# A gated unit's last weights: how its rows are split between a plain load and a gather, and how the gather's pieces are dealt to the DMA engines

## The chip, the cores and the metric

The kernel runs on one core of a Trainium2 chip. Times are device microseconds of one execution. The core has a matrix engine (TensorE, "PE" in the profile, with "PEld" for its weight loads), a vector engine (VectorE, DVE), a scalar engine (ScalarE, ACT), GpSimd (POOL) and SyncE (SP). Data comes from HBM into SBUF, which has 128 partitions, through 16 DMA engines that all queues share.

## The reference

A decode step for eight sequences, D = 512. The row `x` is normalised, then goes into attention over a window of 2048 cached positions (32 query heads, 8 key-value heads of 128) and into a gated unit with F = 1792; the attention's output is scaled by a function of the unit's.

```python
xn = _layernorm(x)                                   # x: 8 x 1 x 512
# A: attention over the last W = 2048 of 8192 positions
q = (xn @ wq) -> 32 heads of 128;  k, v = k_cache[:, :, Sk-W:], v_cache[:, :, Sk-W:]
p = softmax(q . k * 128 ** -0.5);  s = (p . v) @ wo  # wq 512 x 4096, wo 4096 x 512
# B: the gated unit
g = xn @ w_gate;  u = xn @ w_up                      # 512 x 1792 each
b = (sigmoid(g) * u) @ w_down                        # w_down 1792 x 512
out = x + s * silu(b)
```

All data is bfloat16. The caches' windows are 64 MB of the 81 MB that are read.

## The kernel before

One buffer, `ring` (L86), holds nine slots of 16 KB a partition. Every large load goes into slots of it, and all are issued by SP in one order, the list `todo`: a load is issued when a slot is free (`pump`, L89), and `free` (L103) gives slots back when the last reader of a load is recorded. The order is w_gate in two loads, w_up, the last rows of w_down (`want_down`), the gathered rows of w_down (`want_side`), wq, 17 drains of SP's queue, then 32 loads of K and V of 2 MB each (`want_cache`, one sequence and four heads a load, V three loads behind K), then wo in four loads of 16, 10, 4 and 2 rows a partition (`want_rows`).

A load with 128 partitions is split over the 16 DMA engines by partition, eight partitions each, so each engine gets the same bytes of every plain load. w_down is the exception. Its 1792 rows of 1 KB are read in two ways:

- `want_down` (L156) reads the last MT x 128 rows, MT rows to each partition, as one plain load.
- `want_side` (L145) only takes a slot and sets its first SF rows in all partitions to zero (L148, on DVE). The first 64 x SF rows are 64 pieces of SF rows, which one gather by GpSimd (L239) puts into 64 of the 128 partitions. Each partition has an index in `which`; those without a piece have one that is out of bounds, and nothing is read for them.

Which partitions get a piece is said by `SEGS`: triples of first partition, count and step (L139). `sel` (L211 to L219), a 64 x 128 matrix of zeros and ones, is made from them on GpSimd, a copy for each triple; a matmul with `ranks` turns it into the indices (L229 to L238).

The unit is computed at the start: `g_ps` (L323) and `u_ps` (L339) on PE, `h_bf` on DVE (L346), then MT + SF transposes of it (L358), MT of 128 rows and SF of 64. The transposed columns of the pieces are brought to the pieces' partitions by a matmul with `sel` (`spot_ps`, L398), and MT + SF matmuls `d_ps` (L403) give the unit's output, the partitions without a piece adding zeros. In between stand the projection `q_ps` (L387) and after it the heads' layout (L417 to L422).

Then the loop over sequences: K tiles are transposed on PE (`kT_ps`, L484) and copied by DVE (L489), scores (`s_ps`, L502), softmax, transposes of p (L591), values (`o_ps`, L612). At the end 32 steps of four matmuls `fin_ps` (L372) with wo's rows, two DVE operations (L756, L758) and the store by SP and ACT (L760).

Of the kernel before, what the change touches and what calls it, by code (L numbers as in the profile page):

```python
# [10 lines left out]
def kernel(  # L11
# [91 lines left out]
    def free(t):  # L103
        empty.extend(t[1])
        pump()

    def room(k, n, *shape):
        size = 1
        for x in shape:
            size *= x  # L110
        x = ring[:, k : k + n].rearrange("p s e -> p (s e)")[:, :size]
        if len(shape) == 2:
            x = x.rearrange("p (r n) -> p r n", r=shape[0])
        return x, list(range(k, k + n))
# [18 lines left out]

        todo.append((n, f))

    MT = 9
    SF = 10
    NSEL = 64
    SEGS = [(0, 15, 1), (16, 3, 1), (28, 18, 1), (48, 2, 1)]  # L139
    SEGS += [(60, 8, 1), (68, 6, 4), (92, 8, 1), (124, 4, 1)]  # L140
    m0 = NSEL * SF
    assert sum(n for _, n, _ in SEGS) == NSEL and m0 + MT * P == F
    side = {}

    def want_side(w):  # L145
        def f(k):
            t, where = room(k, 1, SF, w.shape[1])
            nc.vector.memzero(t)  # L148
            side["t"] = t
            rows_of[("side", 0)] = (t, where)  # L150
            for r in range(SF):
                weights[("wd_sb", MT + r)] = t[:, r]

        todo.append((1, f))

    def want_down(w):  # L156
        def f(k):
            t, where = room(k, 1, MT, w.shape[1])
            q0.dma_start(
                out=t.rearrange("p t n -> p (t n)"),  # L160
                in_=w[m0:, :].rearrange("(p t) n -> p (t n)", t=MT),
            )
            rows_of[("wd_sb", 0)] = (t, where)
            for r in range(MT):
                weights[("wd_sb", r)] = t[:, r, :]
# [47 lines left out]
    at = 0  # L213
    for p, n, step in SEGS:
        nc.gpsimd.tensor_copy(
# [25 lines left out]
        out_offset=None,  # L241
        in_=B_w_down[:m0, :].rearrange("(p t) n -> p (t n)", t=SF),
        in_offset=bass.IndirectOffsetOnAxis(ap=which[:, :1], axis=0),
# [42 lines left out]

    hT_sb = work.tile([P, MT + SF, Z], bf16, name="hT_sb")
    nc.gpsimd.memzero(hT_sb[:])
# [63 lines left out]
    free(rows_of[("wu_sb", 0)])  # L352
    hT_ps = ps_m.tile([P, MT + SF, B], bf16, name="hT_ps", tag="m")
    cuts = [h_bf[:B, m0:F].rearrange("b (p t) -> b t p", t=MT)[:, t] for t in range(MT)]
# [441 lines left out]
```

## Time and profile before

| | us |
|---|---|
| median of 3 runs | 198.49 (198.38 to 198.54) |
| the profiled execution's own time | 198.86 |
| its span, first to last instruction | 197.08 |
| PE busy | 163.4 |
| DVE busy | 125.7 |
| ACT busy | 40.8 |
| POOL busy | 9.1 |
| mean granted TensorE clock | 0.972 of full |
| bytes read | 81.67 MB, 414 GB/s over the span |

The profile is of one execution, so its durations are summed against that execution's own time. Stages are given in microseconds from the span's start. Beside the page, the trace holds a record of every DMA packet (queue, start, duration, bytes) and of every step of a DMA's completion semaphore, sixteen for a load, one from each DMA engine; neither says which of the sixteen it was.

### The profile page before, as it was taken

The page shows a single profiled execution, that of the slowest core. Times are in us where ns is not written, and L with a number is a line of the kernel's source. Part 1 is how long each engine was busy: PE and PEld are TensorE (multiplying, and loading weights), DVE is VectorE, ACT ScalarE, POOL GpSimd, SP SyncE. Part 2 cuts the span into 40 slices and gives each one's busy share as a digit, 9 for nine tenths or more (in the row PEclk, how much of TensorE's full clock was granted, in tenths as well). Part 3 has the DMA queues.
Part 4 walks back from the last instruction along what each step waited for, and adds up shares of the span by engine and source line. Part 5 has one row for each costly group of instructions (what it writes and reads, how often), then busy time and mean ns, then how long its engine had stood idle before and what let it go on. Part 6 is the DMA issues. An engine that isn't in the chain of part 4 may idle for free.

```text
span 197.1 us, 4818 instructions
## 1 busy us (share of the span) xinstructions
PE 163.4 (83%) x2114; PEld 106.8 (54%) x2114; DVE 125.7 (64%) x247; ACT 40.8 (21%) x95; POOL 9.1 (5%) x31
## 2 busy tenths in 40 slices
PE   0029859999699999799979987999799998878883
PEld 0013423876576575456646654665467566655652
DVE  4540401999799796679667966796549878935201
ACT  0053003001701501600160016001600070071000
POOL 7910000000000000000000000000000000000000
PEclk9999966999999999999999999999879999999999
DMA  6999999999999999999999999999999999999990
GB/s 203 438 440 463 416 406 426 436 436 432 424 429 429 422 426 422 439 432 432 426 432 434 426 426 421 429 436 426 419 442 439 426 431 422 426 429 429 420 401 16
DMA packets 6148, 81.32 MB, mean 413 GB/s; under 512 B 808, under 2 KB 816, under 8 KB 1328
## 3 DMA queue, kind: packets, MB, share of 16 engines
q1 hardware_dynamic: 5936, 80.35, 96.0%
q0 software_dynamic: 144, 0.66, 0.8%
q8 instruction: 16, 0.26, 0.5%
q14 instruction: 4, 0.03, 0.0%
q10 hardware_dynamic: 48, 0.01, 0.0%
HBM read 81.67 MB, written 0.01 MB: 414 GB/s over the span
## 4 chain that ended last, share of the span: by engine, by line
DMA 65%; PE 25%; DVE 5%; ACT 3%; issue 1%; SPq 0%; ACTq 0%
DMA ring<-in_A_k_cache_dram 29%; DMA ring<-in_A_v_cache_dram 13%; PE kT_ps L484 13%; DMA ring<-in_A_wq_dram 11%; DMA ring<-in_A_wo_dram 10%; PE s_ps L502 4%; PE o_ps L612 3%; DMA ring<-in_B_w_gate_dram 3%; DVE kT_sb L489 2%; PE q_ps L387 2%; ACT p_buf L522 2%; PE fin_ps L372 1%; PE d_ps L403 1%; DVE pT_sb L596 1%; ACT L522 1%
## 5 line engine op out<-in xcount | busy, mean ns | idle before, releaser
L489 DVE COPY kT_sb<-kT_ps 128x1024 bf16<-128x1024 bf16 x128 | 84.3, 684 | 26.0 <-PE kT_ps L484 21.2
L484 PE MATMUL kT_ps<-perm,ring 128*128 128x128 bf16 x1024 | 73.4, 221 | 2.0 <-DMA ring<-in_A_k_cache_dram 2.0
L484 PEld LDWEIGHTS <-ring 128*128 128x128 bf16 x1024 | 59.5, 99 | 24.6 <-issue 18.3
L612 PE MATMUL o_ps<-ring,pT_sb 128*32 128x256 bf16 (+1 forms) x352 | 36.6, 330 | 6.6 <-DMA ring<-in_A_v_cache_dram 5.6
L502 PE MATMUL s_ps<-kT_sb,qm_sb 128*32 128x512 bf16 x256 | 25.8, 393 | 1.3 <-DVE kT_sb L489 1.1
L522 ACT ACTIVATE p_buf<-s_ps,st 32x512 bf16<-32x512 f32 x32 | 21.7, 679 | 15.5 <-DVE st L515 15.1
L612 PEld LDWEIGHTS <-pT_sb 128*32 128x32 bf16 (+1 forms) x352 | 12.4, 102 | 19.4 <-issue 17.6
L632 ACT ACTIVATE o_sb<-o_ps,fac 128x512 f32<-128x512 f32 (+1 forms) x8 | 4.9, 608 | 60.5 <-PE o_ps L612 60.5
L596 DVE COPY pT_sb<-pT_ps 128x1024 bf16<-128x1024 bf16 x16 | 10.8, 676 | 1.8 <-PE pT_ps L591 1.8
L502 PEld LDWEIGHTS <-qm_sb 128*32 128x32 bf16 x256 | 7.0, 93 | 8.1 <-issue 1.5
L591 PE MATMUL pT_ps<-turn_rows,p_buf 128*128 128x128 bf16 x128 | 10.7, 227 | 0.0
L591 PEld LDWEIGHTS <-p_buf 128*128 128x128 bf16 x128 | 9.4, 148 | 0.2 <-issue 0.2
L278 PE MATMUL xnT_ps<-ident,xn_bf 8*128 8x8 bf16 x4 | 0.3, 174 | 9.9 <-DVE xn_bf L267 9.9
L549 ACT ACTIVATE w_row<-w 1x128 f32<-1x128 f32 x8 | 2.5, 308 | 28.6 <-DVE w L542 28.6
L346 DVE TENSOR_TENSOR h_bf<-sig,u_ps 8x448 bf16<-8x448 f32 x4 | 2.4, 608 | 6.6 <-PE u_ps L339 6.1
L422 DVE COPY qm_sb<-qT_ps 128x128 bf16<-128x128 bf16 x2 | 1.4, 876 | 8.1 <-PE qT_ps L417 8.1
L323 PE MATMUL g_ps<-ring,xnT_sb 128*8 128x448 bf16 x16 | 5.7, 541 | 0.3 <-DVE xnT_sb L285 0.3
L522 ACT ACTIVATION_READ_ACCUMULATOR p_buf<-s_ps,st 32x1 f32 x32 | 5.9, 184 | 0.0
L515 DVE TENSOR_REDUCE st<-s_ps 128x1 f32<-128x512 f32 x8 | 5.5, 682 | 0.5 <-PE s_ps L502 0.5
L278 PEld LDWEIGHTS <-xn_bf 8*128 8x128 bf16 x4 | 0.2, 114 | 10.0 <-DVE xn_bf L267 10.0
L387 PE MATMUL q_ps<-ring,xnT_sb 128*32 128x512 bf16 x32 | 3.6, 629 | 2.4 <-DMA ring<-in_A_wq_dram 2.4
L642 PE MATMUL m_ps<-ident_f,o_sb 128*128 128x32 f32 x40 | 5.2, 272 | 0.0
(97 smaller groups left out, 97.0 us busy)
## 6 DMA issues: line engine op xcount, KB each, us to landing
ring<-in_A_k_cache_dram SPq DMA_DIRECT2D x16, 2048.0 KB, 28.5
ring<-in_A_v_cache_dram SPq DMA_DIRECT2D x16, 2048.0 KB, 30.4
ring<-in_A_wq_dram SPq DMA_DIRECT2D x1, 4096.0 KB, 21.6
ring<-in_A_wo_dram SPq DMA_DIRECT2D x1, 2048.0 KB
ring<-in_B_w_gate_dram SPq DMA_DIRECT2D x2, 896.0 KB, 6.0
ring<-in_B_w_up_dram SPq DMA_DIRECT2D x1, 1792.0 KB, 13.1
ring<-in_A_wo_dram SPq DMA_DIRECT2D x1, 1280.0 KB
ring<-in_B_w_down_dram SPq DMA_DIRECT2D x1, 1152.0 KB
```

The costliest lines, as they stand in the source:

```text
L323: nc.tensor.matmul(g_ps[:], lhsT=xnT_sb[:, kt, :B], rhs=weights[("wg_sb", kt)][:, k * FC : (k + 1) * FC], start=(kt == 0), stop=(kt == KT ...
L387: nc.tensor.matmul(q_ps[e][Z * g : Z * (g + 1), :], lhsT=xnT_sb[:, kt, :], rhs=weights[("wq_sb", kt)][:, c0 : c0 + D], start=(kt == 0), st ...
L484: nc.tensor.transpose(out=kT_ps[:, c, :], in_=k_sb[:, j * CU + h * CH + c, :], identity=perm[:],)
L489: nc.vector.tensor_copy(out=kT[(b, u)][:, h * CH : (h + 1) * CH, :], in_=kT_ps[:])
L502: nc.tensor.matmul(s_ps[b][NR * l : NR * (l + 1), :], lhsT=qm_sb[:, b, i * G + l, o : o + Z], rhs=t[:, :, PG * l : PG * (l + 1)], start=(u ...
L515: nc.vector.tensor_reduce(out=st[b][:], in_=s_ps[b][:], axis=AX.X, op=ALU.max, negate=True)
L522: nc.scalar.activation(out=p_buf[b % 2][rows, :, l, :], in_=s[rows, :].rearrange("k (c p) -> k p c", p=PG), func=AF.Exp, bias=st[b][rows, ...
L591: nc.tensor.transpose(out=pT_ps[:, c, :], in_=p_buf[b % 2][:, :, :, h * CH + c].rearrange("k p l -> k (p l)"), identity=turn_rows[:],)
L596: nc.vector.tensor_copy(out=pT[b][:, h * CH : (h + 1) * CH, :], in_=pT_ps[:])
L612: nc.tensor.matmul(o_ps[r] if b < WIDE else o_ps[r, 0:2], lhsT=pT[b][:, c, r], rhs=x, start=(c == 0), stop=(c == CU - 1), tile_position=(0 ...
L632: nc.scalar.activation(out=o[:, :n], in_=o_ps[:, :n], func=AF.Copy, scale=fac.pop(b)[:])
L642: nc.tensor.matmul(oT_ps, lhsT=o[:, e, :], rhs=sel[:, e], start=(e == 0), stop=(e == n - 1),)
```

## The change

MT goes from 9 to 8 and SF from 10 to 12: the plain load has 8 KB a partition (1024 rows), and the gather 64 pieces of 12 KB (768 rows). The triples of `SEGS` are new as well: other partitions receive the pieces, and GpSimd makes nine copies into `sel` in place of eight.

```diff
-    MT = 9
-    SF = 10
+    MT = 8
+    SF = 12
     NSEL = 64
-    SEGS = [(0, 15, 1), (16, 3, 1), (28, 18, 1), (48, 2, 1)]
-    SEGS += [(60, 8, 1), (68, 6, 4), (92, 8, 1), (124, 4, 1)]
+    SEGS = [(0, 21, 1), (24, 1, 1), (28, 18, 1), (48, 2, 1), (60, 3, 1)]
+    SEGS += [(64, 5, 1), (72, 5, 4), (92, 6, 1), (124, 3, 1)]
     m0 = NSEL * SF
     assert sum(n for _, n, _ in SEGS) == NSEL and m0 + MT * P == F
```

If the partitions are taken in runs of four, each run with the one 32 partitions above it (0-3 with 32-35, 4-7 with 36-39, up to 28-31 with 60-63; then 64-67 with 96-99 and so on), there are sixteen sets of eight partitions. In that order the pieces are dealt

- before: 8 8 8 5 5 0 0 8, 8 1 1 1 1 1 1 8, of 10 KB
- after: 8 8 8 6 6 1 1 7, 6 1 1 1 1 1 1 7, of 12 KB

All that depends on MT and SF follows: 20 transposes and 20 `d_ps` matmuls in place of 19, `spot_ps` with 96 columns in place of 80, a zeroed slot of 12 KB a partition in place of 10. The order of SP's loads, the loop over sequences and everything behind it are the same.

## The prediction

> **What bounds the kernel now.** I read the page's slices and DMA queues first, then the stages, the waits of SP's queue, the end of the chain, and at last the trace's own records of DMA packets.
>
> ```profile
> span 197.1 us, 4818 instructions
> ...
> DMA  6999999999999999999999999999999999999990
> ...
> q1 hardware_dynamic: 5936, 80.35, 96.0%
> q0 software_dynamic: 144, 0.66, 0.8%
> q8 instruction: 16, 0.26, 0.5%
> q14 instruction: 4, 0.03, 0.0%
> ```
>
> The second line is the busy share of the 16 DMA engines in 40 slices: full from the second slice to the last but one. Below are packets, MB and share by queue: SP's loads (q1), the gather (q0), and 20 fetches of instructions (q8 and q14). The stages tell the same (columns: window, length, busy time and count of each engine, TensorE clock, DMA share, GB/s):
>
> ```profile
> 24.00:60.00 36.00, 30.91 (x419) 21.55 (x420) 24.87 (x47) 7.17 (x17) 0.00 (x0) 0.91 1.00 426
> 60.00:120.00 60.00, 55.33 (x692) 35.39 (x693) 45.96 (x89) 12.88 (x32) 0.00 (x0) 1.00 1.01 431
> 120.00:192.00 72.00, 65.33 (x907) 44.01 (x908) 44.93 (x95) 15.74 (x41) 0.00 (x0) 0.98 1.00 426
> 192.00:197.00 5.00, 1.92 (x60) 1.55 (x54) 0.56 (x2) 0.00 (x0) 0.00 (x0) 0.94 0.07 24
> ```
>
> DMA share is 1.00 until 192 us. The chain of waits gives PE 25%, but SP's waits for PE cost nothing, as the next lines show (who waited for whom, total, times, longest; then a DMA's size and its time to landing):
>
> ```profile
> SPq L172 <- PE kT_ps L484: 105.9, 23, 8.4
> ```
> ```profile
> ring<-in_A_k_cache_dram SPq DMA_DIRECT2D x16, 2048.0 KB, 28.5
> ring<-in_A_v_cache_dram SPq DMA_DIRECT2D x16, 2048.0 KB, 30.4
> ```
>
> A 2 MB load takes each engine 4.86 us (8 packets of 16 KB, 607 ns from start to start) but lands 28.5 us after issue: over 23 us of earlier loads stand before it. A slot freed some tenths later is not felt. The end:
>
> ```profile
> 171.83 19.82 DMA ring<-in_A_wo_dram
> 191.65 0.04 issue
> 191.69 2.24 PE fin_ps L372 x64
> 193.93 0.02 issue
> 193.96 0.29 DVE prod L756
> ```
>
> The last matmuls follow the last pieces of wo. So the time is the end of the slowest DMA engine plus 3.6 us of tail (last landing 193.48, span 197.08).
>
> **The sixteen engines, one by one.** Packet records have no engine number, but an engine's next packet starts 4 ns before its last one's stated end, so I followed the sixteen rows from the load of wq to the end. In steady state all run alike: 607 ns for 16 KB, 381 for 10 KB, 343 for 9 KB, hence 36.8 ns a KB and 4 ns a packet. Only fetches break a row: a q8 fetch delays its engine 1.42 us (gap 0.91, next packet 1.1 instead of 0.61), the four small q14 fetches in the span 0.56 to 0.84. The 16 q8 fetches go round eight engines, two each.
>
> Wq's completion packets fall in classes: 23.61 and 23.70; six from 23.97 to 24.90; 25.33 and 25.38; six from 26.57 to 27.27. If the 128 partitions are taken in runs of four, each with the run 32 above it, the sixteen sets hold 0 (two sets), 1 (six), 5 (two) and 8 (six) pieces of before, and 381 ns a piece gives just these distances. So such a set is an engine's (E0 holds partitions 0-3 and 32-35, E8 those from 64, and so on), and the eight engines of 0 or 1 pieces are those that bear the q8 fetches. Dealing by eight neighbours would give no class of six eights, so that the change would not do what it says is ruled out.
>
> The rows end (last completion packet) at: class 0, 191.86 and 191.95; class 1, 191.99, 192.22, 192.23, 192.31, 192.43 and **193.14**; class 5, 191.38 (one small fetch) and 192.42 (two); class 8, 191.98, 192.06, 192.23, 192.30, 192.68 and 192.89 (one small fetch). The mean is 192.25, so perfect dealing could gain 0.89 us and no more. The 193.14 was already 0.65 behind its class when wq landed, and the landings of w_gate show two engines late from the first load (7.83 and 8.07, the others 7.04 to 7.58).
>
> **What the change moves.** The large load: 8 packets of 8 KB for 9 KB on each engine, 8 x 37 = 0.30 us less. A piece: 456 ns for 381. So E0-E2 (8 pieces, still 8): 8 x 0.075 - 0.30 = +0.31. E3, E4 (5 to 6): 6 x 0.456 - 5 x 0.381 - 0.30 = +0.54. E5, E6 (0 to 1): +0.16. E7, E15 (8 to 7): -0.15. E8 (8 to 6): -0.61. E9-E14 (1, still 1): -0.22. Total bytes are the same.
>
> Now the ends: the late engine of class 1 goes to 193.14 - 0.22 = 192.92; that of class 5 with two small fetches to 192.42 + 0.54 = 192.96; class 0 to 192.1 at most; the rest of class 1 to 192.2. Class 8 depends on which of the six is which, and the records do not tell (three of six each way). Its last, 192.89, becomes 192.28 as E8, 192.74 as E7 or E15, 193.19 as E0, E1 or E2; the next, 192.68, at most 192.98. I take E7, E8 or E15 for the 192.89, half of the cases and the only ones in which its piece count changes; the class-5 engine is then last, 192.96 against 193.14: **-0.19 us**. With E0 to E2 it is +0.05 (rival 1); both ends stay in the range.
>
> Off the path, costed at nothing: **the start.** DVE's memzero writes 3072 instead of 2560 words, 2192 ns x 1.2 = +0.44, and `which` behind it (ends 3.58) and the gather's issue (3.88) wait for it; POOL's ninth copy into `sel` (0.13) ends before that. On POOL the memsets behind the issue move too; their last waits for DVE until 14.29 anyhow. The gather's packets (8.24 to 15.2) alternate with w_up and w_down, whose queue goes on to 24 us, so no engine idles; its reader `d_ps` comes at 31.39. Without this cover: 0.44. **The unit.** One transpose more (19 took 1.7 us, so 0.09), one d_ps matmul (1.80/19 = 0.09), 96 instead of 80 columns in the small copies: 0.2 to 0.3 us on PE and ACT at 23 to 33 us, ahead of the K transposes, which the 23 us of queued loads hide; without them 0.3. SP issues the same DMAs in the same order. **Fetches.** Four more PE instructions in some 4200 move q8 fetches by at most 0.2 us. The 16th (191.07) cost its engine 0.91; at 1.42 that engine ends at 191.99 - 0.22 + 0.51 = 192.28. A 17th would need some 260 PE instructions behind it, and 132 follow.
>
> The profiled run took 198.86, 1.76 beside its span; the median is 198.49. With -0.19: 198.67 profiled, **198.30** as the median.
>
> **Rivals.** (1) The small fetch at 103.5 us sits on E0, E1 or E2, which now carry 96 KB of pieces: end 193.19, +0.05, 198.54. For it: three of six; against: nothing in the rows but that E7, E8 and E15 are as many. [...] The trace shows the late ends, but no slower packets on any engine (4186 of 4224 of 16 KB take 611 ns). (2) Slower: the late start is not tied to one engine and falls on the class-5 engine with two small fetches: 192.96 + 0.65 = 193.61, +0.46, **198.95**. It decides from a lag of 0.19 (no gain), and is past 0.2% from 0.59. For it: the lag comes from first packets of 0.4 to 1.9 us, which look like chance; against: four runs of before within 0.5 us, and one engine in sixteen. (3) Faster: the start is even, and one of the two fetches on that class-5 engine (0.84) goes elsewhere or misses the span: its end 192.12, class 1 at 192.27, class 8 decides at 192.6: -0.54, **197.95**. (4) Before as a rule has no late class-1 engine outside the profile: then 192.89 was last, and after 192.96: +0.07, 198.56.
>
> **How the numbers follow.** This kernel's measurement can tell about 0.2%, 0.4 us, from no change. Forecast 0.32 (198.30, its own range 198.1 to 198.45); rival 1 0.20, less than the forecast as it needs the heaviest three; rival 4 0.10; rival 2 and its like (late start on a heavily dealt engine) 0.13; rival 3 and its like (the after's starts fall better) 0.25. The forecast and rivals 1 and 4 stay within 0.2%, less 0.04 for what 0.2 us of scatter adds past the bound, on both sides: faster 0.27, same 0.58, slower 0.15. The range takes in rival 3 and most of rival 2: 197.85 to 198.85.
>
> **What would show it.** Gather packets of 12 KB at 456 ns and w_down packets of 306; the first gather packet 0.4 us later; wq's completion still in classes, of 1, 6, 7 and 8 pieces, the heavy ones 3.2 us behind the light; 16 q8 fetches; last landing near 193.3. Wrong would be: an engine idle between 24 and 190 us, a 17th fetch before 192, or a last engine of another class than I named.

## The result, and the profile after

The median went from 198.50 us (22 runs, 198.24 to 198.77) to 198.79 us (22 runs, 198.63 to 199.09): ratio 1.0016, 95% interval 1.0010 to 1.0023. The change made the kernel slower by 0.3 us; the forecast was 0.2 us faster.

The two profiled executions say the opposite. The page of after, queues and slices as above:

```profile
span 196.8 us, 4823 instructions
...
DMA  6999999999999999999999999999999999999990
...
q1 hardware_dynamic: 5936, 80.22, 95.9%
q0 software_dynamic: 144, 0.79, 1.0%
q8 instruction: 16, 0.26, 0.5%
q14 instruction: 4, 0.03, 0.0%
```

The span is 0.2 us shorter, 0.13 MB has gone from SP's queue to the gather's, and the fetches are the same 20. The stages and SP's waits have not moved (columns as above):

```profile
60.00:120.00 60.00, 55.45 (x696) 35.50 (x693) 46.04 (x89) 12.80 (x31) 0.00 (x0) 1.00 1.01 429
120.00:192.00 72.00, 65.56 (x917) 44.11 (x918) 44.90 (x95) 15.82 (x41) 0.00 (x0) 0.98 1.00 426
```
```profile
SPq L172 <- PE kT_ps L484: 105.6, 23, 8.4
```

The DMA engines are still full to 192 us (DMA share 1.01 and 1.00). The chain ends on the last landing again, 193.26:

```profile
193.26 0.02 issue
193.28 0.41 PE fin_ps L372 x8
193.69 0.02 issue
193.72 0.29 DVE prod L756
```

The contradiction is in the choice of executions. The profiled run of before took 198.86, above every one of its 22 timed runs; that of after took 198.63, the lowest of its 22. So both kernels were profiled once more (the two rows "again" below), and every run's packets were followed as in the prediction.

In all fourteen profiles the kernel's time is the last packet of the slowest DMA engine plus 5.68 to 5.82 us. From wq's last packet to the end each engine takes the same in every run, to 0.03 us (one engine of `c2_e1_e3` took 0.1 longer): 165.41 without a fetch, 165.95 to 166.01 with one small fetch, 167.09 with two, 168.24 with two large ones. On one engine, E10, the second large fetch starts in all fourteen profiles just as its last load ends, 166.82 behind wq, and itself ends at 167.74. Where two rows of packets ran in step and could be exchanged, these sums told which was which. The engines are numbered as in the prediction (E0 has partitions 0-3 and 32-35). The first profile of after shows the same sets of partitions: wq's last packets stand at 23.49 to 24.21 us in eight rows and at 25.82 to 27.39 in the other eight, as eight sets have one piece and eight have six to eight. E1 is the one with the small fetch at 103.5 us, E3 the one with two small fetches, E9 the one that started late in the first profile; the first experiments knew E1 and E3 by their fetches only, and `b1_both` shows how the numbers were found. Times in the table are from the span's start, the last one in bold.

| last packet, us | E1 | E3 | E9 | latest of the others | profiled time |
|---|---|---|---|---|---|
| before, first | 192.89 | 192.42 | **193.14** | 192.68 | 198.86 |
| before, again | **192.86** | 192.69 | 192.50 | 192.30 | 198.64 |
| after, first | **192.95** | 192.92 | 192.43 | 192.80 | 198.63 |
| after, again | **193.25** | 193.02 | 192.32 | 192.50 | 198.96 |
| a1_sizes | **192.99** | 192.51 | 192.17 | 192.56 | 198.67 |
| a2_deal | 192.58 | 192.89 | **192.96** | 192.39 | 198.69 |
| a3_e012_7 | 192.54 | **193.19** | 192.52 | 192.66 | 198.87 |
| a4_e34_5 | **192.96** | 192.47 | 192.78 | 192.52 | 198.64 |
| b1_both | 192.52 | **192.68** | 192.29 | 192.56 | 198.37 |
| b2_e34_7 | 193.03 | **193.57** | 192.29 | 192.42 | 199.26 |
| c1_best | 192.01 | 192.15 | 192.26 | **192.87** | 198.67 |
| c2_e1_e3 | **192.49** | 192.48 | 192.48 | 192.49 | 198.21 |
| c3_e0_e2_e3 | **193.00** | 192.46 | 192.77 | 192.44 | 198.80 |
| c4_before_e1 | 192.29 | 192.73 | **192.92** | 192.84 | 198.74 |

### The profile page after: what moved, and what is told of

Same layout as the page of the kernel before. It is cut to its first block, busy times and chain, and to the rows that moved or that the text cites. A ratio compares the mean times of both kernels' runs of the same rounds, so it can differ in the third digit from the quotient of the medians.

```text
span 196.8 us, 4823 instructions
## 1 busy us (share of the span) xinstructions
PE 163.2 (83%) x2116; PEld 106.7 (54%) x2116; DVE 126.2 (64%) x247; ACT 40.8 (21%) x95; POOL 9.2 (5%) x32
## 4 chain that ended last, share of the span: by engine, by line
DMA 65%; PE 25%; DVE 5%; ACT 3%; issue 1%; SPq 0%; ACTq 0%
DMA ring<-in_A_k_cache_dram 29%; DMA ring<-in_A_v_cache_dram 13%; PE kT_ps L484 13%; DMA ring<-in_A_wq_dram 11%; DMA ring<-in_A_wo_dram 10%; PE s_ps L502 4%; PE o_ps L612 3%; DMA ring<-in_B_w_gate_dram 2%; DVE kT_sb L489 2%; PE q_ps L387 2%; ACT p_buf L522 2%; PE fin_ps L372 1%; DVE pT_sb L596 1%; PE d_ps L403 1%; ACT L522 1%
```

## The experiments

Each edit below is against after, but for `c4_before_e1`, which is against before. From `a3_e012_7` on only the added lines are shown; they take the place of the two lines of `SEGS`. Each run is compared with runs of before on the same chip.

**The two halves of the change.** `a1_sizes` has after's sizes and before's dealing:

```diff
-    SEGS = [(0, 21, 1), (24, 1, 1), (28, 18, 1), (48, 2, 1), (60, 3, 1)]
-    SEGS += [(64, 5, 1), (72, 5, 4), (92, 6, 1), (124, 3, 1)]
+    SEGS = [(0, 15, 1), (16, 3, 1), (28, 18, 1), (48, 2, 1)]
+    SEGS += [(60, 8, 1), (68, 6, 4), (92, 8, 1), (124, 4, 1)]
```

> New sizes (8 rows by the plain load, pieces of 12 rows), pieces dealt as before: 8 8 8 5 5 0 0 8, 8 1 1 1 1 1 1 8. Before is 198.50, after 198.79. Theory 1, the last engine is that of E0 to E2 which bears the small fetch at 103.5 us: its load is the same as after's (+0.31 on before), 198.8. Theory 2, the last engine is that of E3 and E4 with two small fetches (5 pieces of 12 KB for 5 of 10, less 8 KB of plain load: +0.08): 198.5 to 198.6. Theory 3, the larger zeroed slot and gather delay the start: 198.8.

198.67 against 198.47, ratio 1.0013 (1.0004 to 1.0022): most of the loss, with E1 last. `a2_deal` has before's sizes and after's dealing:

```diff
-    MT = 8
-    SF = 12
+    MT = 9
+    SF = 10
```

> Old sizes (9 rows, pieces of 10 rows), pieces dealt as after: 8 8 8 6 6 1 1 7, 6 1 1 1 1 1 1 7. Theory 1: E0 to E2 carry what they carry before, 198.5. Theory 2: E3 and E4 have one piece more, +0.38 on an engine that was near the end, 198.8. Theory 3: 198.5, as gather and zeroed slot are the old ones.

198.65, ratio 1.0006 (0.9997 to 1.0015), between the two theories. Its packets have E3 raised to 192.89, E1 left at 192.58, and E9 last. Neither theory has it alone.

**One late group relieved at a time.** `a3_e012_7` takes a piece each off E0, E1 and E2:

```diff
+    SEGS = [(0, 22, 1), (24, 2, 1), (28, 7, 1), (36, 3, 1), (40, 3, 1), (44, 2, 1)]
+    SEGS += [(48, 2, 1), (60, 3, 1), (64, 5, 1), (72, 6, 4), (93, 6, 1), (124, 3, 1)]
```

> After, with one piece taken from each of E0, E1 and E2 (7 7 7) and given to E5, E6 (2 each) and E8 (7). Theory 1: these three end 0.46 earlier, and the next, E3 or E4 with two small fetches, sets the end some 0.23 earlier than after: 198.55. Theory 2 and theory 3: nothing changes, 198.8.

198.74, ratio 1.0015 (1.0006 to 1.0024): no gain on after, against theory 1. E1 did end 0.4 lower, 192.54, but E3 stood at 193.19. `a4_e34_5` does it the other way:

```diff
+    SEGS = [(0, 22, 1), (24, 2, 1), (28, 17, 1), (48, 1, 1)]
+    SEGS += [(60, 3, 1), (64, 5, 1), (72, 6, 4), (93, 5, 1), (124, 3, 1)]
```

> After, with one piece taken from each of E3 and E4 (5 each) and given to E5 and E6 (2 each); E0 to E2 keep 8. Theory 1: 198.8. Theory 2: 0.46 less on the last engine, 198.5 or lower. Theory 3: 198.8.

198.62, ratio 1.0007 (0.9998 to 1.0016): E3 is down at 192.47 and E1 stays at 192.96; a part of the loss may be gone, as the interval holds 1 but ends at after's 1.0016. Both engines had become late, and relieving one leaves the other: the next runs call this theory 4.

**Both relieved, and the engines told apart.** `b1_both`:

```diff
+    SEGS = [(1, 6, 1), (8, 8, 1), (19, 3, 1), (25, 2, 1), (28, 15, 1), (44, 2, 4)]
+    SEGS += [(49, 3, 1), (60, 9, 1), (73, 3, 5), (92, 7, 1), (116, 2, 5), (124, 4, 1)]
```

> After's sizes, with both late groups relieved: E0 to E2 7 each, E3 and E4 5 each, E5 and E6 2 each, E7 8, E8 7, E9 to E14 1, E15 8; within an engine the piece-less partition differs, so that the packets tell which engine is which. Theory 4 (both the small-fetch engine of E0 to E2 and the two-fetch engine of E3 and E4 had come to about 193.0, so that relieving one alone leaves the other): both go to about 192.54, the end is then set by the engine of E9 to E14 that starts late, about 192.6 to 192.8; 198.2 to 198.4, faster than before. Theory 3 (larger zeroed slot and gather cost the time whatever the dealing): 198.7 to 198.8.

198.31 against 198.37 on the same chip, ratio 0.9996 (0.9987 to 1.0005): the loss is gone with sizes, gather and start as in after, which ends theory 3. The time is in the range that was expected, but the gain on before did not come, and E9 was not the last engine: it ended at 192.29, E3 at 192.68. In the gather, a partition without a piece still has a packet, of 4 bytes (in before and in after the gather has 64 full packets and 80 of 4 bytes, 64 for such partitions and 16 for the steps of its semaphore); the order of full and empty packets in each row names its engine: the small fetch at 103.7 us is in the row whose fourth packet is empty, E1; the fetches at 51.7 and 121.9 are in E3's row, the one at 157.1 in E4's. The large ones go round E11, E12, E13, E14, E5, E6, E9, E10, twice. E0, E2, E7, E8 and E15 bear none.

**The price of a piece.** `b2_e34_7` puts a seventh piece on E3 and E4:

```diff
+    SEGS = [(0, 21, 1), (24, 2, 4), (29, 18, 1), (48, 3, 1)]
+    SEGS += [(60, 2, 1), (64, 5, 1), (72, 6, 4), (93, 5, 1), (124, 2, 1)]
```

> After, with one piece more on each of E3 and E4 (7 each), taken from E7 and E15 (6 each). Theory 4: the two-fetch engine goes from about 193.0 to 193.45, and being last it moves the time by nearly a whole piece, 0.35 to 0.46: 199.15 to 199.25. Theory 3, and any in which an engine's last packet does not set the end: 198.8.

199.21, ratio 1.0038 (1.0024 to 1.0051), 0.0022 or 0.44 us above after's: that is one 12 KB piece, 0.456 by the packets, on an engine that is last. The end of its chain:

```profile
193.91 0.01 issue
193.92 0.41 PE fin_ps L372 x8
194.34 0.02 issue
194.36 0.29 DVE prod L756
```

It is after's chain, all of it 0.64 us later, as E3's last packet is (193.57 against after's last, 192.95). In this one profile E3 ended 0.65 later than its own 192.92 in after: 0.46 by the piece, the rest by a later start.

**Both kernels again.**

> The kernel before once more, for its packets: how far behind its class does the late engine of E9 to E14 start (0.65 in the first profile)? If the lag is of that execution alone, this one ends near 192.9, set by the small-fetch engine of E0 to E2; if it belongs to the engine, 193.1 again. By the first, the comparison of the two first profiles flattered the change by some 0.25.

> The kernel after once more, for its packets: theory 4 expects the last two ends to be the small-fetch engine of E0 to E2 and the two-fetch engine of E3 and E4, both at 192.9 to 193.2, and the late engine of E9 to E14 below them.

E9 ended at 192.50 in before this time and E1 was last in both, 192.86 and 193.25: +0.39, where the packets' arithmetic has +0.31 and the 44 timed runs +0.29. The chains, before again and after again:

```profile
193.18 0.02 issue
193.19 0.41 PE fin_ps L372 x8
```
```profile
193.57 0.02 issue
193.58 0.41 PE fin_ps L372 x8
```

**Which engines, with few pieces.** `c2_e1_e3` moves two of the 64 pieces, `c3_e0_e2_e3` three:

```diff
+    SEGS = [(0, 21, 1), (24, 2, 4), (29, 10, 1), (40, 5, 1), (48, 3, 1)]      # c2
+    SEGS += [(60, 3, 1), (64, 5, 1), (72, 6, 4), (93, 6, 1), (124, 3, 1)]
+    SEGS = [(0, 22, 1), (24, 2, 4), (29, 6, 1), (36, 7, 1), (44, 2, 4)]       # c3
+    SEGS += [(49, 2, 1), (60, 3, 1), (64, 5, 1), (72, 6, 4), (93, 6, 1), (124, 3, 1)]
```

> After, with two of the 64 pieces moved: one off E1 (7) and one off E3 (5), to E4 (7) and E8 (7). Theory 4: E1 and E3 both go to about 192.55 and nothing else is near; 198.3 to 198.4. If it takes more than these two engines: above 198.55.

> After, with one piece each off E0, E2 (7) and E3 (5), to E4, E8 and E5; E1 keeps its 8. Theory 4: E1 with its small fetch still ends at 193.0 to 193.2; 198.6 to 198.75, although three pieces have moved where the run above moves two. If any of E0 to E2 could be the late one: 198.4 or between.

On one chip, with 198.52 before: 198.41 (ratio 0.9999, 0.9990 to 1.0008) and 198.65 (1.0009, 1.0000 to 1.0018). Two pieces, off E1 and E3, undo the loss: the interval lies below after's 1.0010 to 1.0023. Three off the neighbours of E1 and off E3 leave E1 at 193.00; by the times alone that run lies between the two.

**Beyond before.** `c4_before_e1` takes a piece off E1 in before, `c1_best` deals after's pieces by the map of fetches:

```diff
+    SEGS = [(0, 15, 1), (16, 4, 1), (28, 11, 1), (40, 6, 1)]                  # c4: MT = 9, SF = 10
+    SEGS += [(48, 2, 1), (60, 9, 1), (72, 6, 4), (93, 7, 1), (124, 4, 1)]
+    SEGS = [(0, 22, 1), (24, 2, 1), (28, 10, 1), (40, 4, 1), (48, 2, 1)]      # c1: MT = 8, SF = 12
+    SEGS += [(60, 8, 1), (72, 2, 1), (76, 3, 4), (92, 7, 1), (124, 4, 1)]
```

> The kernel before, with one piece of 10 KB moved from E1 (7) to E4 (6). Theory 4: E1 goes from 192.7 to 192.9 down to 192.3 to 192.5, and E3, E8 or the late one of E9 to E14 set the end, 192.5 to 192.8: 0 to 0.2 us faster than before, 198.25 to 198.45.

> After's sizes, dealt by the fetches that the packets of the earlier runs showed on each engine (E3 two small ones, E1 and E4 one, E5, E6 and E9 to E14 two large ones, E0, E2, E7, E8 and E15 none): 8 6 8 4 6 2 2 8, 7 0 2 1 1 1 0 8. Theory 4, by the sum of load and fetches on each engine: E1 and E3 end at 192.1, E0, E2, E7 and E15 at 192.3 to 192.6 become last: 198.1 to 198.25, faster than before by 0.1 to 0.2%. If instead a cost outside the engines' sums holds the end: 198.4 or more.

198.55 (ratio 1.0004, 0.9995 to 1.0013) and 198.53 (1.0002, 0.9993 to 1.0011): no difference that these runs tell, and both forecasts missed. In c4, E1 came down to 192.29, but E9 was late again, 192.92, and an engine with eight pieces ended at 192.84. In c1, E1 and E3 ended close to where the sums put them, 192.0 and 192.1, but two of the engines with eight pieces and no fetch had begun late and ended at 192.68 and 192.87. The sums took every start at its mean; a late start takes the place of what is evened out. No version was measured to beat before; the lowest ratio is that of b1, 0.9996, whose interval holds 1.

## Why the prediction was wrong

**The sums of each part held.** Gather packets are 12 KB and take 456 ns from start to start (stated 460), w_down's 8 KB packets 305; 16 large and four small fetches came, and no 17th large one; from 28 to 190 us no row of packets idles but for gaps of 0.30 to 0.95 us at the fetches. Two small readings were off without moving the sum: 36.8 ns a KB is per 1000 bytes (607 ns for 16 KB, less the 4 a packet, is 37.7 per 1024), and the 16th fetch cost its engine's loads nothing, since it starts as the last of them ends (191.07 us in before, 190.88 in after). The zeroing grew as costed, and the gather's issue moved with it. Before, then after (start, duration, engine, line, instruction, and what it waited for):

```profile
1.34 2.19 DVE L148 MEMSET ring<- 128x2560 uint32 x1 [1.34 <-PEq L780]
...
3.88 1.17 POOL L239 DMA_INDIRECT ring<-in_B_w_down_dram,which  x1 [0.70 <-DVE which L231]
```
```profile
1.45 2.62 DVE L148 MEMSET ring<- 128x3072 uint32 x1 [1.45 <-PEq L780]
...
3.98 0.10 DVE L231 TENSOR_SCALAR which<-rank_ps 128x1 uint32<-128x1 f32 x1
```
```profile
4.38 1.17 POOL L239 DMA_INDIRECT ring<-in_B_w_down_dram,which  x1 [1.11 <-DVE which L231]
```

The zeroing took 2.62 us for 2.63 forecast, and the gather was issued at 4.38 in place of 3.88. b1 has the same zeroing, the same transposes and matmuls, and no loss: these are covered, as forecast.

**E3's step was right:** 0.54 was forecast for it, 192.96 its end; it ended at 192.92 and 193.02. That it came so close is partly luck, as E3's end in before was 192.42 in one profile and 192.69 in the other.

**The step that failed first is the choice within class 8.** I had put the small fetch of 103.5 us on E7, E8 or E15 by counting cases. It is on E1, which after loads with 8 x 12 KB: rival 1's mechanism, +0.31 on that engine, where the forecast had it lowered by 0.15 or 0.61. The argument behind the count (only there does the number of pieces change) said nothing of where the fetch is. By that trace the six engines could not be told apart; the 0.46 to 0.92 between the answers was larger than the change forecast.

**The step that turned the sign is the baseline.** The sum was made against an end that E9's late start had set, 193.14. Over the fourteen profiles E9's wq ends 0.15 to 0.85 us behind the mean of E11 to E14 (with equal pieces), about 0.5 on average; the first profile of before has the 0.85, the largest. With E9 less late, as in the second profile of before, E1 is last on both sides and the change costs it 0.31. That is rivals 1 and 4 together, which the prediction priced one at a time (198.54 and 198.56) and never added: 198.49 + 0.31 = 198.80, the measured 198.79. How the miss divides can be estimated from the medians, less a tail of 5.72 us as in the profiles: before ended at about 192.78, 0.36 under the 193.14 that the sum started from, and after at about 193.07, 0.11 over the forecast 192.96. So the baseline is the larger part. The warning was in the numbers shown: the profiled run was 0.37 above the median, which is more than the whole change, and the prediction carried its difference over to the median as if both ended on the same engine. The stated range, 197.85 to 198.85, did take in 198.79, but it was wide enough for either sign and says nothing for the mechanism.

Which engine usually ends the runs of before is not shown. With its sizes E9 was last in three profiles of four (the first, `a2_deal` and `c4_before_e1`), and a piece less on E1 in c4 did not gain anything that the runs tell; E1 and E9 seem to be about level there. After's E1 and E3, on the other hand, are shown as the cause of the loss: a piece off both undoes it (b1, c2), while with one of them relieved the other ends last, and all or about half of the loss is left (ratios 1.0015 in a3, 1.0007 in a4, 1.0009 in c3).

**The late ends are not of slower packets.** A 16 KB packet took 611 ns on every engine (4186 of 4224 packets in each of the first two profiles; the others took up to 621, or 858 to 1159 beside a fetch), no fetch fell on E7, E8 or E15 (b1), and the late end with the small fetch is E1's.

## What to carry to other kernels

Here the DMA engines were busy to the end (DMA share 1.00 or 1.01 in every stage from 24 to 192 us), and in all fourteen profiles the time was the last packet of the slowest of the sixteen plus 5.68 to 5.82 us. Where a profile shows the same, judge a change of a few KB on that engine alone. Find out by the packets what else each engine bears (here, instruction fetches that held one up by 0.55 to 1.42 us) before dealing work over them. A profile is one execution: where it lies apart from the median by more than the effect, its last engine need not be the usual one, so sum against several engines that are close to the end, and add up rivals that can hold at once.

## What the runs showed of the hardware that I had not expected

A fetch of instructions took its time from one of the sixteen engines that carry the loads, and held it up by more than its own packet took: 1.42 us for 16 KB (0.88 to 0.97 its own packet), 0.55 to 0.84 for 8 KB (0.31). The engine was the same in all fourteen profiles: large fetches went round the eight engines named, and the four small ones fell on E3, E1, E3 and E4 each time. Behind wq, an engine's time repeated to 0.03 us from run to run, but for the 0.1 in c2; nearly all scatter was in the first 27 us, where engines with equal loads differed by up to 0.9 us when wq landed (23.97 to 24.90 in the first profile of before). Why E9 is behind in every profile (0.15 to 0.85 us), and others in some, stays open: it was not tried.
